# A new written-out instruction order and new PSUM banks for a fused conformer block

## The chip, the cores and the metric

The kernel runs on one core of a Trainium2 chip. The metric is device time in microseconds (us) of one launch; lower is better. A profile of one execution stands beside the times. Engines: TensorE (PE, with its weight loads PEld), VectorE (DVE), ScalarE (ACT), GpSimd (POOL), and SyncE (SP), which only issues transfers.

## The reference

One conformer block on x of shape (2, 4000, 144) in bf16, with 4 heads of 36 and a depthwise convolution over 5 steps:

```python
x = x + 0.5 * (silu(layernorm(x) @ w_ff1a) @ w_ff1b)          # 144 -> 576 -> 144
q, k, v = split_heads(layernorm(x) @ w_qkv)
p = softmax(q @ k.T * 36 ** -0.5)                             # 4000 x 4000 for each batch and head
x = x + merge_heads(p @ v) @ w_o
a, b = split(layernorm(x) @ w_pw1)
c = depthwise_conv(a * sigmoid(b), dw)                        # 5 taps along time
x = x + silu(c) @ w_pw2
x = x + 0.5 * (silu(layernorm(x) @ w_ff2a) @ w_ff2b)
return layernorm(x)
```

## The kernel before, in words

**Tiling.** The 8,000 tokens are cut into 16 chunks of 500 (eight to a batch), a chunk into 4 blocks of 125 tokens. A chunk's queries meet the keys of its batch in tiles of 64 keys. One score tile holds 64 keys of four heads by 500 queries, as four 64x64 matmuls side by side in the array (PS<-QT,KT), which fill two PSUM banks. Its exponent is taken in one of two ways: on ScalarE, one ACTIVATE Exp of 128x1000 (PT<-PS); or on VectorE, by arithmetic on the bits in five instructions (two PT<-PS 128x500 to int16, two PT<-PT 128x1000 on uint16, one PT<-PT product). The matmuls with V (PS<-PT,VA, 64x37) add into two PSUM banks of their own (6 and 7); one column of ones gives the softmax sum. A "q" matmul in the program is one of these 64-row quads, "f" is one with the full array.

**Around the attention.** Before a chunk can be attended, its first feed-forward (PS<-XT,WA; tanh on ScalarE, TH<-PS; product on VectorE, HT<-TH,PS; PS<-WB,HT; residual on VectorE, X<-PS,X), a layer norm and the projections to Q, K and V (PS<-XTQ,WQ and so on, copies QT, KT, VA) must be done. After a chunk's attention come the epilogue (QT<-PS, transposes with IDF, AN<-PS,RD), the output projection, a layer norm, the gated product (U), the convolution (PS<-U,DG, then SW), a projection, the second feed-forward and the last layer norm, whose XN is stored (out_dram<-XN).

**A layer norm** is bn_stats on VectorE (ST<-X), then seven instructions on GpSimd in the middle of the run: a TENSOR_SCALAR RS<-ST, a power RS<-RS,NHALF, a TENSOR_SCALAR RS<-ST, and four XN<-X,RS. At the start and the end of the run VectorE or ScalarE makes XN. A 32x32 transpose on VectorE (XN<-XN) and two sets of transfers through DRAM (rows<-XN, four transfers; XT<-rows or XTQ<-rows, two) turn it to columns. GpSimd also copies the edges of U between chunks (U<-U).

**Order.** A planner in the program (`Sched`, `pick` and the loop at the end) walks through all this work and records every instruction with its dependences; each step of the planner makes a block of instructions on one engine. `Rec.op` keeps, for each instruction, what it reads and writes. Then `Rec.reorder(ORDER)` puts the blocks of each engine into another order: `ORDER` has one string for each engine, and the i-th character is how many places the i-th recorded block goes forward or back (P is 0, Q is +1, O is -1; `~` begins a longer form). `PLACES` has one digit for each PSUM tile, the bank of six (0 to 5) in which it lies, or the first of a pair. `Rec.place` reads it. Waits are put in afterwards, by `reorder` and `finish`, from the dependences that the order leaves open, a tile's bank being free when the tile before it in that bank has been read. Each engine and SP then run their own list strictly in order: an instruction that waits holds all behind it on its engine.

```python
            for i, blk in enumerate(blocks):
                assert at[i + shift[i]] is None
                at[i + shift[i]] = blk
            lines[e] = [o for blk in at for o in blk]
```

All instructions are issued from one line of the program (L419 in the profile), so groups are told apart by their tiles.

Of the kernel before, what the change touches and what calls it, by code (L numbers as in the profile page):

```python
# [44 lines left out]
        "LMNLPRPKWOYFMNOVNOHXXMKOLNNNN[[_MMMTLLTKKKLJOOPRP`MO_OMNOMPQLLMRMMMPPPQOSYP[MOOISOLNPPIPSPTOLRNNWPNO"
        "QQMMPUQRN[QQQRJFPPPPJQQSPPKQQNPPPPVPPQOPVXOOPNDNPRROSVSYNFWMPYUPNDPJFPNPTOPYOLOPNQ[NLNRPMRLNNOPhUNZM"
        "MMNLNNPMMWYLPNZKNLMF[LPPSLVINLNOMWQNYPYPLQHKOSNORPGPPPS[OOLOOPPYLNNNVOMNOM^QMNTOO_KMMNOMPPLPNQOYL]RY"
        "LMKLMMPLY]KLNNQXMRXSLI[MDObNOENPMMNSNNQMMWNNNOSVNiKZNNQOTFNNOMXXUMMMM?TLLIYMQXXLLMMQZMJJ`ORLMUMKQYNL"
        "INPMMUVNLNOMYPMOORNNRUNKPNO_ROQLSSKMQMKPROLPSOORNOSOOOTVNNNNSNTMTMNNOVXNOMORLSNVXIMSYLMKLN^XYNLMNHMM"
        "WLLMXMNYMOLNNXMNXMMVMM[SLJLLZN^OLNNJUbLLLQNLPRGNNOOOPNRNOPPPeOOOOPSOOORROf`OPNO^@QDLJLMOLTKLTMTRKGMQ"  # L50
        "QNUOPNROYYPZOHNbILLLLbTLLSLLLLPLM_M[MMMMMcMMMMNLMOdZMNNNNIMMMMXMNNVOMKMMZNOUaMMMQMM]^HOMKNNNJZMKM[LM"
        "QgLLLMWMMMMU]LLLV^MQJMWTMHBHMZSKL[PLLZTMK_bMMIGbMPLPQMSVCKRKSMBINPPSPVOLOOOOZQNNS[MMMMNSMOMNO]aNNcMM"
        "MMMMMMNLNNNZWNZMZPNKPMYBENOPJYNNPMPQOLQNPPRRO[YQJNOPQOPXFPHPNOOOPWOOOOOOXPMTQOLOK^OXNNOMPPPLPPHQQNgR"
        "cOLQOMPNOOOOdRM@LdOJOIPIOOOJOOOOJOOPNUPNOOQQYLQ]NLZ[LLLdWKIKLLLWULE]LLLLLOMWRcKLLLNZM[PMMRILNKZJ`[JK"
        "MOLLUbKeJLLYKOUKMMMMMY=KMNNZNL^NLNNNNNN_NNNOQQNPTHNN_NLOOO^QMNPKO^QQM_JFPLOPJMNPPLPhMPROOPQOWOWNNNNU"
        "U?NO[HMTOOOCNOOOQO[OQOUOOOPHVORPYMGNPPMOVNN[QOVKPNZPGLOY]OPLOPPPBHOOORPRROR`OPWQNZCLNNPQZKMQETOJOMNU"
        "OOOOOPPPP[OOPNQNQRLMVZLOTNKPLLOOPPVPNOVOMRMOSLOOPPPPPZOWOMNNN]NLMPRTLNZUNLQMNYWNRAOPTOSHRNDQOPTOOPNP"
        "UOUQ_LROQQIQFNOYPNUKQNKTNKOQRSTNQNRXFQOQVQULMVEMPPP[PPPQODZcMPMMQINPKMPNOOOPRMNPPPQOZOOOOOQOMOOPXOOZ"
        "NNNNNN`NPWMXNNOPNKOCNOXPNOQOMZQMUOKXMZP[^XIMMOOKPABPJOPPPXOOQOPPPRIOPSOVSMOTKQUKLPNQNPXQOMROMPMQWQMU"
# [10 lines left out]
    "act": (  # L70
        "PPPPPPPPPPPPPRTNNOOPPQOPPPPPPXPNOSNNNNPPPPQOPPSPNOQZQORKRSLLOQQJPPPPQQNQOPPPPPPPPPQQQMPPQOPPPPPPPPRO"
        "OPQOPQQNPPPPPPPPPPPPPPPPPPPPPPPPPPPPPPPPPPPPPPPPPPPPPPPPPPPPPPPPPPPPPQOPPPROSNOOPPPPPPPPPQOPPPPPPPPP"
        "QOPPPPPPPPPPPQOPPPPPPPPPPPPQOPPPPPPPPPPPRPNPQOPPPPPRPNPPPPPPPPPPPPPPPPPPPPPPPPPPPPPPPPPPPPPPPPPPQOQQ"
        "NPPPPPPPPPPPPPPPPPPPPPPPPPPPPPPPPPPPPPPPPPPPPPPPPPPPPPPPPPPPPPPPPPPPPQOPPPPPPPPPPPPPPQOPPQOPPPPPPPPP"
        "PQOPPPPPPPPPPPPPPPPPPPPPPPPPPPROOPQOPPPPPPPPPPPPPPPPPPPQOPPPPQOPPPPPPPPPPPPPPPPPROOQQQMPPPPPPPPPPPPP"
        "PPPPPQOPPQOPPPPPPPQOPPPPPPPPPPQOPPQOPPPPQQQQQKQQNPPPPPPQOPPPPPPPPPPPPPPPQOPPPQOPPPPPPPPPPPPPPPPPPPPQ"
        "OPPPPPPPTOOOOROOPPPPPPPPPPPPPPPQOPQOPPPPPPPPPPQOPPQOPPPPPPPQOPPPPPPPPPPQOPPPPQOQOPPPPPPPPQOPPPPPPPPP"
        "QOPRPNQOPPPPPPPQOPPPPPPPPPPPPPPPPPPPPPQRNOPPPQOPPPPPPPQQNPPPPPPPPQOPPPPPPPQOQOPPQOPPPPPPPPPPQOPPPPPP"
        "PPPQOQOPPPPPPPPPPPPPPPPPPPPPPPPPQOPQQNPPPPPPPPPPPPPPPPPPPPROOPPPPPPPPPPPQQNPPPPPPPPQOPPPPPPPPPPPPPPP"
        "PPPPPQOPPPPPPPRPNQOPPPPPPPQOPPPPPPPPPPPPQOPPPPPPPPPPPPPPPPPPPPPPPPPPPPPPQOPPPPPPPPPPPPPPQOPPPPPPPPPP"  # L80
        "PPPPPPPPPPPPPPPPPPPPPPPPPPPPPPPPPQOSPNRNOQOUQNPMOPPPRORNQNPPPPPPQOROQQMPPPPPPQOPPPWORNNNOO"
    ),
# [2064 lines left out]
```

## Time and profile before

| what | value |
|---|---|
| runs | 875.77, 875.0, 875.19 us; median 875.19 |
| span of the profiled execution, first to last instruction | 873.9 us |
| its own time beside the span | not listed; the median of the runs is 1.3 us above the span |
| TensorE clock granted | 0.998 of full speed |
| instructions | PE 11,419, DVE 1,821, ACT 1,098, POOL 573 |
| DMA | 28.82 MB, mean 33 GB/s |

A group of the profile is read as: operation, tile written <- tiles read, shape, count, then busy time and mean ns of one, then the idle time just before and what ended it. Records of ScalarE and VectorE overlap a little where one follows another at once. A row of a timeline is start, duration (of a merged run of like instructions), engine, operation. Rows of a stage table give the stretch, its length, then busy us and count for PE, PEld, DVE, ACT and POOL, then granted clock, DMA share and GB/s.

### The profile page before, as it was taken

What the parts mean: (1) busy time and instruction counts of PE and PEld (TensorE: products, weight loads), DVE (VectorE), ACT (ScalarE), POOL (GpSimd) and SP (SyncE); (2) the same over time, 40 slices, a digit from 0 to 9 for tenths busy, and PEclk for the clock granted to TensorE, in tenths of its full rate; (3) what the DMA queues carried; (4) which work ended last, traced back from release to release, by engine and by line L of the source; (5) the groups of instructions that cost most, each with busy time, mean ns of one, the idle gap of its engine ahead of it and who ended that gap; (6) DMA issues with size and microseconds to landing.
All of it is one profiled execution on the core that took longest, in us unless ns stands there. A gap on an engine that the chain in (4) does not pass through costs nothing.

```text
span 873.9 us, 27051 instructions
## 1 busy us (share of the span) xinstructions
PE 844.3 (97%) x11419; PEld 385.8 (44%) x11419; DVE 824.8 (94%) x1821; ACT 845.4 (97%) x1098; POOL 292.8 (34%) x573
## 2 busy tenths in 40 slices
PE   8999999999999999999999999999999999999996
PEld 6543444334444434443444444445444433444465
DVE  7988999999999999999989999899999999999987
ACT  6799999999999999999999999999999999999985
POOL 6750350341325141152211552621314413022434
PEclk9999999999999999999999999999999999999999
DMA  4230101121121020212001120110111011001111
GB/s 100 49 62 29 23 17 44 33 67 30 29 52 39 17 50 11 45 22 47 23 4 29 24 56 17 30 30 16 37 31 24 21 31 21 19 15 38 28 26 35
DMA packets 114353, 28.82 MB, mean 33 GB/s; under 512 B 101090, under 2 KB 114230, under 8 KB 114230
## 3 DMA queue, kind: packets, MB, share of 16 engines
q1 hardware_dynamic: 112646, 26.39, 13.8%
q8 instruction: 90, 1.47, 0.7%
q10 hardware_dynamic: 1584, 0.69, 0.3%
q14 instruction: 33, 0.27, 0.1%
HBM read 13.44 MB, written 13.61 MB: 31 GB/s over the span
## 4 chain that ended last, share of the span: by engine, by line
ACT 59%; PE 25%; DVE 11%; POOL 4%; issue 1%; POOLq 0%; DVEq 0%
ACT PT L419 54%; PE PS L419 25%; ACT TH L419 5%; DVE PT L419 4%; POOL XN L419 2%; POOL RS L419 2%; DVE ST L419 2%; DVE X L419 1%; DVE XN L419 1%; DVE HT L419 1%; DVE U L419 0%; DVE KT L419 0%; DVE RS L419 0%; DVE AN L419 0%; DVE XT L419 0%
## 5 line engine op out<-in xcount | busy, mean ns | idle before, releaser
L419 ACT ACTIVATE PT<-PS 128x1000 bf16<-128x1000 f32 (+1 forms) x818 | 752.0, 1051 | 3.7 <-PE PS L419 2.8
L419 PE MATMUL PS<-QT,KT 64*64 64x500 bf16 x3968 | 419.9, 384 | 12.4 <-ACT PT L419 7.4
L419 PE MATMUL PS<-PT,VA 64*37 64x500 bf16 x4728 | 406.4, 372 | 1.6 <-DVE QT L419 1.0
L419 DVE TENSOR_SCALAR PT<-PS 128x500 int16<-128x500 f32 x380 | 250.2, 668 | 6.9 <-PE PS L419 5.1
L419 PEld LDWEIGHTS PS<-QT,KT 64*64 64x64 bf16 x3968 | 124.8, 104 | 232.0 <-ACT PT L419 132.2
L419 POOL TENSOR_SCALAR RS<-ST 125x4 f32<-125x4 f32 x130 | 37.8, 291 | 475.6 <-DVE ST L419 469.0
L419 PEld LDWEIGHTS PS<-PT,VA 64*37 64x37 bf16 x4728 | 142.7, 96 | 93.4 <-issue 13.6
L419 DVE TENSOR_SCALAR PT<-PT 128x1000 uint16<-128x1000 uint16 x380 | 154.2, 419 | 2.3 <-PE PS L419 1.0
L419 POOL TENSOR_SCALAR XN<-X,RS 125x144 bf16<-125x144 bf16 x260 | 144.7, 586 | 9.7 <-DMA out_dram<-XN 1.5
L419 DVE TENSOR_TENSOR PT<-PT 128x1000 bf16<-128x1000 bf16 x190 | 127.5, 674 | 0.9
L419 ACT ACTIVATE TH<-PS 128x500 bf16<-128x500 f32 (+3 forms) x194 | 102.8, 551 | 4.7 <-PE PS L419 4.5
L419 POOL TENSOR_TENSOR RS<-RS,NHALF 125x4 f32<-125x4 f32 (+1 forms) x93 | 92.8, 1002 | 33.5 <-DVE RS L419 27.9
L419 DVE SCALAR_TENSOR_TENSOR HT<-TH,PS 128x500 bf16<-128x500 bf16 (+1 forms) x135 | 81.0, 613 | 10.1 <-ACT TH L419 9.7
L419 PE MATMUL PS<-XT,WA 80*128 80x500 bf16 (+5 forms) x288 | 74.5, 364 | 4.2 <-DVE XT L419 1.0
L419 DVE BATCH_NORM_STATS2 ST<-X 125x6 f32<-125x288 bf16 x160 | 65.5, 446 | 1.6 <-DMA X<-in_x_dram 1.4
L419 DVE SCALAR_TENSOR_TENSOR X<-PS,X 125x288 bf16<-125x288 f32 (+1 forms) x128 | 56.6, 449 | 5.6 <-PE PS L419 4.3
L419 PE MATMUL PS<-WB,HT 128*125 128x144 bf16 (+1 forms) x640 | 52.6, 230 | 0.8 <-ACT HT L419 0.5
L419 PEld LDWEIGHTS PS<-WB,HT 128*125 128x125 bf16 (+1 forms) x640 | 44.3, 136 | 14.2 <-issue 4.3
L419 PEld LDWEIGHTS PS<-XT,WA 128*128 128x128 bf16 (+1 forms) x288 | 21.1, 97 | 37.7 <-issue 10.1
L419 POOL COPY U<-U 128x2 bf16<-128x2 bf16 (+1 forms) x54 | 12.0, 263 | 56.2 <-DVE U L419 56.2
L419 DVE STREAM_TRANSPOSE XN<-XN 128x320 f32<-128x320 f32 x54 | 27.0, 500 | 2.8 <-POOL XN L419 2.6
L419 PE MATMUL PS<-U,DG 128*128 128x250 bf16 (+6 forms) x204 | 28.8, 263 | 0.1
(95 smaller groups left out, 519.9 us busy)
## 6 DMA issues: line engine op xcount, KB each, us to landing
rows<-XN SPq DMA_DIRECT2D x216, 40.0 KB, 2.0
XT<-rows SPq DMA_DIRECT2D x56, 128.0 KB, 2.0
rows<-AN SPq DMA_DIRECT2D x60, 40.0 KB, 2.0
X<-in_x_dram SPq DMA_DIRECT2D x15, 140.6 KB
XTQ<-rows SPq DMA_DIRECT2D x26, 70.3 KB
out_dram<-XN SPq DMA_DIRECT2D x13, 140.6 KB
XT<-rows SPq DMA_DIRECT2D x56, 16.0 KB, 1.9
out_dram<-XN SPq DMA_DIRECT2D x3, 70.3 KB
```

The costliest lines, as they stand in the source:

```text
L419: ins = getattr(eng, o.name)(*o.a, **o.k)
```

## The change

The two tables get new contents: all five strings of `ORDER` and the digits of `PLACES`. The recorded instructions, their number, their operands except for the PSUM bank, and every other line of the program stay. The new order comes from a re-timing of the recorded program with mean intervals, in which an instruction of GpSimd has a price that depends on what VectorE runs beside it. Each string begins as before. Cut to the beginnings:

```diff
 ORDER = {
     "pe": (
-        "PPPPPPPPQOPPPPROQNPPRQPQLPPRPTPUPNIZOVOKVVL~OOKOK~OUHINSNLMMMOPNOJSOOL[I[KMYMKOGRNJHFKOOOE^NNN_dMKLM"
+        'PPPPPPPPQOPPPPROQNPPQQQRLRPQLSOSQNLYWXMQOXJ~O^JtG~O[IILRKKLLLNOQRRRTMTWCZCQMPAGGc>HKKLMOMG]MMM_gLJKKWbKH?KILDHjafGeGEIoKHNIIaOJJJJKVJKKK_ZJS'
 ...
     "act": (
-        "PPPPPPPPPPPPPRTNNOOPPQOPPPPPPXPNOSNNNNPPPPQOPPSPNOQZQORKRSLLOQQJPPPPQQNQOPPPPPPPPPQQQMPPQOPPPPPPPPRO"
+        'PPPPPPPPPPPPPPRSNNOPPQRNQNPPQOWORNTNLNPPPQRSTTUWIJVRUHLMGNPPQQQMPPPPQQNPPPQOPQQQQQQQQHPPPPPPPPPPPQOQQQMPPPPPPPPPPPPPPPPPPPPPPPPPPPPPPPPPPPPPP'
 ...
     "dve": (
-        "PUO[VM~P6~P6~P)~P6ILIKKLDKMJQRJJJKIKQKKLJKMKOLJWOILJHLJNQNPHFGNNNJMMMMBMWOIKIMINLMNOODNDPSPLORCFVSWC"
+        'PUO[VM~P2~P<~P6~P6ILIKKLDKMJQRJJJKIKQKKLJKMKOLJMMIMKMMJSOKNHIIKLLLLLLLLLWKOKTHYHLMPPPCRCQTPSSS=>SJV>MALRLZB:THHKKLEKKLLEMMJLNKKLOPLMPSOOQDPP'
 ...
     "pool": (
-        "PPPPPPPROOPPPSOPNPQQQQQQJPPPPPP_PPPPPJOOPQ[NKTMMOMNOSNUMNSNRNTKVNVMPLMPMROQTMOOTVMNNNOQTMOOQWMOOOSNN"
+        'PPPPPPPROOPPPROQNPPPPPPQORPQQQQJPPPPPQOPPVQNR[NKMOOOSNUMMPLTNPPQLQORSNRMRMSUMOPSOJOPPPQOPPPPROOPRRNRPLQOQOPPQOPPROQN'
 ...
     "sp": (
-        "PPQOPPPPQOPPPPPPPPPPPPPPWPWMNNNOPLPPPPPPQOPPPPPQRNOPPPPPQOPPQOPPPPPPPPPPPPPPPPPPPPPPPTOPNYNOWNNNNNNN"
+        'PPPPPPPPQOPPPPPPPPPPPQQNRPRMOPPPPPPSOOOPPQOPPPPPROOPPPPPQOPPSOOQNPPPPPROOPPPPPQOROOPPTOPNZNOUNNNNNNOTOTNNNOQOPPUOOOPNPPPPZOOOOOOOPNOPPPPPPPU'
 ...
 PLACES = (
-    "3054320451505435202310543130213550204405323242301405230054110122532155431241204124012410314032034023"
+    '30543204515054352123103401355024221105304541034523052303450014223451310452412041240124103140030241334102432040234013402430043213430243040224'
 ...
```

More of the change, by code (lines that the diff above doesn't have):

```diff
@@ L45 @@
[L45 to L59, printed above, removed]
@@ new lines @@
+        '5KMKCTZUIJ]JHIQ[SMKUGL^KLLMNPQMNOTPQUWJOINNSOPLQSPUOQQIQRUQQQLFQQQMPZPPPLPNOOOOhZORPUMIJMORYKIMNPM_NNRMNGPNQQNLPNUXNSNLNLOQSVOXX^OZ_MNGBGWKI'
+        'LLVPJQIKRNdNSVNLPMfN^MVNNNJMMM?VNNNa^YLDKKLWLZKKO]VJXFJbSLXYJGLQNHWNKWT5KNdXJNaQMULLN@KNTKMMYNLJOVPNOYJOLPYOaRJNPPIaSYOMDOOKOEQNJQRNRPJPPWPZ'
+        'MNNNOMTNNOM]OOOPNRPWX[^MHMOJENJSMNL[TOK_MNUYJMKb_LIMHLLTQMIMKOZKMPMSPNLNOQO]OOOOOQOMQQUMRPYHRPRVOSJE^MKOPNOPPM[^MMMWL[_KKKKKLJQ]aUKKVFKKKLUS'
+        'LJKUMPJPNPRO^TMYPMMJQMMMNNQOTO^OMPQLXPQKPTJOJLQQNXOOOOOZNNNOTNNPMXLOORNNNOVOOQNNU^MNNOTLNNNUUWNLMNZPNUjOMTNL=NRSQNGUOOOOOSDOQNSQIXLOOOOOOOZO'
@@ new lines @@
+        'OOOOUNPMMVYLPNRXJLVOJLW[LLOQJMMPNPRMY[RPKQKKOQNPRPGPPPQUQOLPQQQWJOOOOOZNPNOQNPMOO^bNNNOMO_LPNPJJL]MSLPKKQ`PMWGNLNNOWLX^OLI[NINIMNSMNLMYTNNOM'
+        'N[NNNORVN`OLNNQOUDNNOMZSLMMNSOZNKTLNOUcMNNOTFNNNWMWNLMOMXJXOJNOMNRaNKOPNOPNOOQRMQUMJPNOWQOPXKWQLQLJOQZJOQNNOUOMNNOVTNNNNQMUPWMNNP_LNQ]NQNPMQ'
+        'FZOW^ILHNNOXXGJMZWKK[JJKXLLSKL[LLWKOWLMXLLXYKILM]PT[JHMIQ^[JKUJLWPHLLNGMaPRMWMMNZMMMMMUMMMURMa[OLOPSC`KLMRJLUMJMNTPTLJMQQMYOPNQN]OPUMI`PLMPN'
+        'IWPLOLNNNN_WNNNQMMYLMeMMMMVLMMfMMMMOMSNNNNQSNOEVMNOMTMNW`MPNSNNNGWPNLNOMNSOSNTMNWcMMNNWMMMNSULLLT]M]QMUINCMNNOVIN[TMMTXNJ_`OLTESKLMRLNTV?KXM'
@@ new lines @@
+        'ROSPPEQU[]NDMMOLT^MKNUKINNUZMKMMM`bMMcLLLMMMMMNLNPKUXOSNGZLGQNLSZOVLMIOO[NJSO^KPMPNQNGPUZPNJOQQUGOKPMPPPPfOOOOOQRNLNORVTLaNJ[PLGPNGOZPKLNOPe'
+        'QOSPPJlYNNOMVRL9KcOIPHHRNOMZOOQSNLHMA]NOOOYR`Lb_KKX[JEJd`IEJHLHYTKEPDKKKY]LTZPGLIKL^LWWLLOHLM]aK^JLLcQMJJ`NWHRGMJFUHLLMXXLTIMMMUMKQRMZLOOOOO'
+        'OOOQ`MOQYMMNgNLPPKPQIPSGOZPQO`OGOGLQ^KKPQaPgIPHOPGROWN]NNNNTC>NN[INTOOOGNOOOQOPPPVOOOORNNPRPRMQNPPPS[OO_PPQHNPTYTMOIVQM@WNOPDbNNNQOQQNQ_NOFP'
+        'M^NKOPPQIVMPPGOSPIOaOOOOOOZOO_NOMPPLTPJPA[WOJOZPILNPNP^OFPMOOQTNOKNNPPPPPZOdPMOOKYOLNPJMWOYUQLTMKEWNQBNOPNSSOMNQOPTOOOOPPRZO^^NNNN]MWPCeJN]M'
@@ new lines @@
+        'EPH^C_NIKURLQNKXFGPBXPNYN]GNNKO^WNLQOLS_NOHOOWPR;QQ]KQJ[EXOfNKOHNOZHQGSMPJQKKPLOQQQSQSNPGWRTOPLTNTWQMMPTOVNOYTOWLOVPNWN]U^DNNNQHQ(LMYOOPRUOM'
+        'PNDQOROOPPPUSNORLRUSJOLRMSQRLMSPNQNXOPNRPQTKKPQVQRWOPQFSSO]LQORTOMOOXSNXOPQWRZLQaLOPASOO(KOOOZNNNNTNNUULLVKMXLNOMbN_MMMUQLLLLNX^NIMMOPTMSOCL'
+        'MQOPQOPXRNOMOQRNTPUROMSODOQOPQORUXNLOMNSOMN[PNWNOMRMMMMUVNYMSLLLMXSMMMNQTMTLOM]TOL[XNKSPIYNISQGUSEO_STJUMRPUJK>OMSUOKP[OKQSMRXKLOKNOVRNLQOLX'
+        '[NOMNOVLNLNNTMTVMMMTUSMMIRLQWPLQNNWOMVWNO`[ITIJMTMMNOMDPNQOUOOU_MV`LJMVQIMOIXNU`ENNUNTDGMMMPPSLPTLP_MNPNOSPMYNKYRXN[JRILEKRKQNLQOR_OQLQORKOP'
@@ new lines @@
+        'UPPSLNFXPNVNO]OSJMJPMSNPT`PWJX[_cJCLJKN^KDGLJ]LLNNN[SLFSK^KKLTMNOb^XNKNLMNOM@MNOTPNROHPRVQSPKTRPLGWPN]WNNUNLHMQWXKQ_LMENZKOPQ`NHNSSZWNSIGN@O'
+        'SVJXNUNOMOR`ZLO;cOMKWMYRMKILLPUOL@UMMPNOYaNNNOXTMJ[RKILMHOMX`WLLLMZLLLLNNNSOMUQQXRa]P[TN@EMKOOPNAPGPRXNNVNN^MMMMWQMNLNNNNUUNNPNYTJNSMNL[_QMQ'
+        'INOVPMGQKLMROVROLNO^PMO`NNRNOKOKXTM^JM^VLHMPRLNDXNS`N[DMNNOPNOPNAPQLSO^OSSOOLHQOMQOQRPJQRPMSQRRTTTOHRRTRPRSQRTRCSVP9QJNQRPQKPQSPPQRUOTGUN]PL'
+        'QHPRKvMMNRSLRMJMRNOMOPPQQNSSNRMRLCNPNPNOOOOUPNOOOPPPQOPQO'
@@ L69 @@
+        ''
     ),
     "act": (
-        "PPPPPPPPPPPPPRTNNOOPPQOPPPPPPXPNOSNNNNPPPPQOPPSPNOQZQORKRSLLOQQJPPPPQQNQOPPPPPPPPPQQQMPPQOPPPPPPPPRO"
[L72 to L75, printed above, removed]
@@ new lines @@
+        'PQOPPPQOPPQOPPQOPPPPPPPPPPPPPPPPPPPPPPPPPQOPPPPPPPPPPPPPPPPPTOPPQQKQQQMPPPPPPPPPPPPPPQOPQQNPPPPPQOPPPPPPPPPPPPQOPQQNPROQQQQQQIQQNPPPPPPPPPPP'
+        'PPPPPPPPPPPPQOPPPSORNNPPPPPPPPPPPPPPPPQQNPPPPPPPTOPNOROOPPPPPPPPPPPPPPPPPPPPPPPPPPPPPPQOPPQOPPPPPPPQOPPQQNPPPPPQOPPPPRORNOPPPPPPPPPPPPPQOROQ'
+        'NPPSQNNPPPQQQQQQJQOPQQNQQQMPPPPPPPPPPPQOSOOQQQLPPPPPPPPQOPPPPPPPPPROOPPPPPQOPQOPPPPPPPPPPPPPPPQOPPPPPPPPPPPPPPPPPPPPPPPPPPPPPPPPPPQQQMPQQNPP'
+        'PPPPPPPPPPPPPPPPPPPPPQOPPPPPPPPPQQNPPPPPPPPQOPPPPPPPPPPPPPQQNPPQQQMPPPPQQNRPNQOPQOPPPPQOPPPPPPPPPPPQRNQQQLPPQOPPPQQQQLPPPPPPPPPPPPPQRPQLPPPP'
@@ new lines @@
+        'OREQNQQNQSQOSQOQVVWOPNKN@OPQOPQOROORRNNQOPQOSSPNQTPPPRSQUMQQRR>QQQQQQEPPWOOOPNOOVPNOPNVNOOOOOQOPUOOVNNNORNSMPNQOPPSPSMPMPPPPPPRPNPPPPVOQUMVO'
+        'PLPPRPEPQO[OTOMOMNQOUOKTOQ[MJOOOOOOOPTUOKVPQKPJQNQRRORPRRSURLNRRNQQQQQQQQQQQSQRTQZPQTQGPRPWJP#PPRVQWQQNWHPNBOOOQOPSOOOROOXOiNOROMNRHNPRLNNPN'
+        'SNNNNSNNNPWOOOOOPQQQQQQHP`SNNNNOOPNOOTOMO[RKNNOOOTNPTRVOVHHOMNTNOOOQOPPPPPPPQSNPNPWROMTMOMNPQOPSOOOQOQOPPQSQOLQOPROQQMPPPPQQNPPSSNNRMQNPPRPQ'
+        'QLPRRRN]PJOPNOOOOOOOQOQOPQOPPPPPPQOSOPNPPPQOPPTRWMMQLWOLRMVMUVKLNLMOdSPPLLOOWNNOMOMNNOPQMPPTPNPNPPQRPMPRSOMQNQQNRPNRORNOPPPPPPPPPUOPNROMRfNP'
@@ new lines @@
+        'MSOSNKMUMO]OMNORNFMMTOURKLPLQOPRTNSMRMMPPPPPROQNSPNOPPPPPPQOQOTOSTMNLOPSOOOPROOQOSOOOQOPPgPNOPNRSNTKNSJMULTLMMNLPROOROVNOOOPQMPPPPPPUQNPMOXP'
+        'PMOOOUOMPNTNOOOPQOYOOOTOMNNNPPQQQSPRJQRPKPPUPNPPMQQNTOPRTNQOSVROUDKNNOPPQOPPPPPPPQQNPRORNOQOPQOPPQRNRNRRMTQTRJUKROJVPSPTOQTTPHTRPLTRS<MMTOPP'
+        'MQOQOSORRRLZQOPQRNOPROSVR>NLPQMPQORPNPPPPPPQOQOVOOPNPNPPRPQQRPRTWPSSPSWSQRRSVRYQ?7O?QQNQQJPPPPPPPQOPQOPROhQOPROOQGNPNOOOOPPPRPJMOPPPRPNROOPP'
+        'QOUQNQOLPQOPPQOPQQRMOSPUQRZSIPTHOIQMQSKTNPMOPPPVOPXOOOQOHRNNQRTOLPNRYQVQOQQUSFSEIMRRRMQLWSNNQMSQURIKTOLOSNPNQOQOROOPROQNPQSPMRPMTQSZM[PRKUMV'
@@ L105 @@
+        ''
     ),
     "sp": (
-        "PPQOPPPPQOPPPPPPPPPPPPPPWPWMNNNOPLPPPPPPQOPPPPPQRNOPPPPPQOPPQOPPPPPPPPPPPPPPPPPPPPPPPTOPNYNOWNNNNNNN"
-        "VOWNNNNPMOPVOZNOMNNOOSNNNPPZOPNOOOOOOOPQSNOOPPQQN"
+        'PPPPPPPPQOPPPPPPPPPPPQQNRPRMOPPPPPPSOOOPPQOPPPPPROOPPPPPQOPPSOOQNPPPPPROOPPPPPQOROOPPTOPNZNOUNNNNNNOTOTNNNOQOPPUOOOPNPPPPZOOOOOOOPNOPPPPPPPU'
+        'VNNNNNOPPPPPPPROO'
+        ''
     ),
@@ new lines @@
+    '52305240425042105245024504250425042504250424052404250425023504250324302350243034203530143025243054204403250424052505320524054205320524502405'
+    '24052404250424052505250424052405240253003414314002254411240124210412041204131043103420532033051035103515301035130402430243024301430143034210'
+    '43013402430342034201340315401320341204021402140214021402143104140134021402140214021401340214012042104310431043104212403154301140124240204214'
+    '12041204021402104213412041204120412024230034243024310430243024502352130340214021411341040043214021402140214021401340214020412041104331340214'
@@ new lines @@
+    '12041214013401340214020412140204102402141200421025052504205240441330052502401214023401340101305224120402140204120412041204124124120041134021'
+    '43425301503510351341043141204203532034013401340214012043025301530153015301530130104502431004321403153013010032143024301404302430243020425431'
+    '04002431340234023410241334013410431330105301530153015031003513513234011340104331043141042041104310430143013531043310431041204313401340120412'
+    '04120412041204013402140214024024303420243024302430342034203402340234024030232430523055310430234032404204350425024025054204203450320525042044'
@@ L130 @@
+    '24052505240520305312030542045204250524052504240420524052504240504225043251403034202403430242104303402235042034203430235024203430242034034203'
+    '24023520350235103104253413401350235024302430204313401042341204120402014021420402140240124121412040214102402140423040323413561445520322602013'
+    '24143254105304421103341250153354054253016503'
 )
```

65 lines of the change are left out of this document (11 added, 54 removed).

## The prediction

> **What bounds the kernel now.** I read the profile page first, then the busy time by stage, the waits of each engine, and the timeline where an engine falls short. The page:
>
> ```profile
> span 873.9 us, 27051 instructions
> PE 844.3 (97%) x11419; PEld 385.8 (44%) x11419; DVE 824.8 (94%) x1821; ACT 845.4 (97%) x1098; POOL 292.8 (34%) x573
> ACT 59%; PE 25%; DVE 11%; POOL 4%; issue 1%; POOLq 0%; DVEq 0%
> ```
>
> Three engines are nearly full, and the chain that ended last runs 59% through ScalarE (ACT), 25% through TensorE (PE), 11% through VectorE (DVE) and 4% through GpSimd (POOL). The same instructions run after the change, so a gain can only come out of idle time, stretched instructions or TensorE's changes of array shape. By stage (time, PE, weight loads, DVE, ACT, POOL busy):
>
> ```profile
> 17.00:50.00 33.00, 30.49 (x320) 16.45 (x317) 31.15 (x81) 27.81 (x50) 23.65 (x49) 1.00 0.23 48
> ...
> 75.00:540.00 465.00, 457.16 (x6306) 196.80 (x6308) 447.66 (x949) 462.20 (x571) 145.08 (x277) 1.00 0.15 32
> 540.00:565.00 25.00, 23.47 (x300) 10.37 (x292) 21.61 (x46) 24.43 (x33) 17.36 (x28) 1.00 0.09 18
> 565.00:825.00 260.00, 252.39 (x3499) 109.75 (x3495) 252.85 (x529) 259.93 (x321) 72.20 (x143) 1.00 0.12 26
> ...
> 840.00:874.00 34.00, 26.82 (x318) 23.03 (x315) 28.02 (x102) 22.14 (x58) 11.84 (x16) 0.95 0.13 33
> ```
>
> From 75 to 825 us ScalarE shows 2.80 + 0.57 + 0.07 = 3.4 us without work. The room lies at the ends: 5.2 us in 17 to 50, and 11.9 us after 840.
>
> ```profile
> PE PS L419 <- ACT PT L419: 8.3, 30, 0.5
> PE PS L419 <- DVE PT L419: 2.1, 7, 0.8
> ```
>
> These are TensorE's waits between 50 and 840 us (total, times, longest). They are waits for a PSUM bank that the exponent on ScalarE, or VectorE's exponent, has not yet read. So in the middle TensorE and ScalarE hold each other, and speeding up one alone is only partly paid.
>
> **The change, part by part.** I read the shift tables against the blocks of the kernel before. At another place stand 2,307 of 2,855 blocks on TensorE (median two places), 270 of 1,093 on ScalarE, 1,250 of 1,689 on VectorE, 72 of 125 on GpSimd and 76 of 157 on SP; 409 of 1,724 PSUM tiles get another bank. Matched with the instructions of the trace, the first 16.9 us stay as they are.
>
> *Changes of array shape on TensorE.* Counting neighbours in the two orders, matmuls of another kind (64-row quads beside full-array ones, or the small V forms) follow each other 768 times before and 746 times after, 22 fewer. The price:
>
> ```profile
> 406.49 0.38 PE L419 MATMUL PS<-QT,KT 64*64 64x500 bf16 x4
> 406.70 0.38 PE L419 MATMUL PS<-PT,VA 64*37 64x500 bf16 x4
> ...
> 410.00 0.41 PE L419 MATMUL PS<-QT,KT 64*64 64x500 bf16 x4
> 410.34 0.59 PE L419 MATMUL PS<-XTQ,WK 72*128 72x500 bf16 x2
> 410.90 0.41 PE L419 MATMUL PS<-QT,KT 64*64 64x500 bf16 x4
> ```
> ```profile
> L419 PE MATMUL PS<-XTQ,WK 72*128 72x500 bf16 (+1 forms) x68 | 19.2, 366 | 0.0
> ```
>
> Four quads take 0.21 us when quads follow (406.49 to 406.70) and 0.34 when a full matmul follows: 0.13 for the change. Back, two full matmuls step by 0.59 - 0.37 = 0.22 each, 0.44 in all, and the quads come after 0.56: 0.12, which may hold a wait. So 22 x 0.125 = 2.75 us less on TensorE. What covers it: ScalarE, wherever the chain does not run through TensorE. I take the chain's 25%, -0.7 us; ends -2.75 and 0. The Trainium skill, TensorEngine Tiling (Array Packing), section Key Properties, says that changing the tiling mode drains the engine. The skill's TensorE: Matmul & The Clock Gate, section Step-by-step, counts 128 cycles for a drain, which at 2.4 GHz gives an estimate of 0.053 us and 1.2 us for the 22, against 2.75 by the rows; the measured rows decide here.
>
> *The stretch from 17 to 50 us.* ScalarE's waits there, and the chain:
>
> ```profile
> ACT TH L419 <- PE PS L419: 2.8, 5, 1.4
> ACT PT L419 <- PE PS L419: 1.0, 2, 0.8
> ACT XTQ L419 <- PE PS L419: 0.6, 2, 0.3
> ACT VA L419 <- PE PS L419: 0.6, 1, 0.6
> ```
> ```profile
> 17.29 1.01 POOL RS L419
> ...
> 29.67 0.50 POOL XN L419
> 30.21 0.51 DVE XN L419
> ...
> 38.58 8.00 PE PS L419 x90
> ```
>
> GpSimd carries the chain from 17 to 30 us and its order is unchanged up to 35 us, so those 13 us stay. Behind them the new order brings the copies of XTQ, K and Q on ScalarE forward by 5 to 11 places and puts tanh blocks back by 1 to 7; on TensorE the long run of 92 full-array matmuls is broken up, with quads in between; the exponent that waited 0.8 us changes places with the next. Of the 5.0 us waited I take that 0.8 and a little more, -1.0. Ends: -5.0 (all of it) and +1.4, once more the longest wait seen there, since the tanh blocks put back feed VectorE. The large memset of U2 moves five places back on GpSimd; the work it then stands behind is not on the chain after 38.6 us, so it costs nothing, and its own reader comes later than 50 us.
>
> *The GpSimd pile-up at 543 us.* Four layer norms stand there in a row, with VectorE beside the first:
>
> ```profile
> 544.56 1.57 POOL L419 TENSOR_SCALAR RS<-ST 125x4 f32<-125x4 f32 x1
> 546.23 2.79 POOL L419 TENSOR_SCALAR XN<-X,RS 125x144 bf16<-125x144 bf16 x4
> ...
> 559.50 0.23 POOL L419 TENSOR_SCALAR RS<-ST 125x4 f32<-125x4 f32 x1
> 559.84 1.87 POOL L419 TENSOR_SCALAR XN<-X,RS 125x144 bf16<-125x144 bf16 x4
> ```
> ```profile
> 544.71 0.74 DVE L419 TENSOR_SCALAR PT<-PT 128x1000 uint16<-128x1000 uint16 x2
> ...
> 545.37 0.67 DVE L419 TENSOR_TENSOR PT<-PT 128x1000 bf16<-128x1000 bf16 x1
> ```
>
> The same 125x4 operation takes 1.57 us beside VectorE's PT passes and 0.23 without; four XN take 2.79 against 1.87. The change swaps the third and the fourth layer norm, so the fourth, on the chain, ends some 4.3 us sooner, and the third, which feeds a store, later. SP gets that store into the gap in which it waits for rows to land:
>
> ```profile
> 562.28 2.55 SPq L419 DMA_DIRECT2D rows<-XN  x4
> 566.23 0.82 SPq L419 DMA_DIRECT2D XT<-rows  x2
> ```
>
> Behind it on SP stand the XT loads; the store's input would end by about 562, before the load could go at 566, so it holds nothing up. At stake is ScalarE's 0.57 us of this stage; I take -0.4; ends -0.57 and +0.5 should the store's layer norm come later than that.
>
> *The rest of the middle.* Nothing but a shuffle by a place or two; each of the queues, SP's 76 moved blocks of two or four DMAs included, has the order of its inputs nearly as before. At stake are 2.87 us of ScalarE's idle time; I take -0.5; the loss end is the first rival below.
>
> *The tail.* On VectorE the four XN of one store move eleven places back, behind the last residuals, and three residuals of other chunks 15 to 48 places back:
>
> ```profile
> 864.57 1.00 DVE L419 TENSOR_SCALAR XN<-X,ST,RS 125x144 bf16<-125x144 bf16 x4 [0.22 <-POOL RS L419]
> 867.40 0.45 DVE L419 SCALAR_TENSOR_TENSOR X<-PS,X 125x288 bf16<-125x288 f32 x1
> 869.36 0.55 DVE L419 TENSOR_SCALAR XN<-X,ST,RS 125x144 bf16<-125x144 bf16 x2 [0.75 <-POOL RS L419]
> ```
> ```profile
> 866.35 0.84 PE L419 MATMUL PS<-WB,HT 128*125 128x144 bf16 x10 [0.34 <-ACT HT L419]
> ```
>
> The last residual could start at 867.19 instead of 867.40: -0.2. The moved 1.0 us then fills the 0.75 us that VectorE waits before its last XN, so its excess, +0.25, lands on the end, and its store leaves with the last ones. Taken as 0; ends -1.5 and +1.5 (the 1.0 us and half a microsecond of store, or the same won by the deferred residuals).
>
> **Sum.** -0.7 - 1.0 - 0.4 - 0.5 + 0 = -2.6 us on a span of 873.9. The median of the runs, 875.19, lies 1.3 above the span for what stands around it; I carry that over: 872.6 us, 0.3% faster.
>
> **Rivals.**
> *Score tiles behind VectorE (slower).* Of 818 score tiles, 167 were written into a bank that a VectorE instruction had last read; with the new banks 181 are, 14 more. Such a wait costs 2.1/7 = 0.3 us in the row above. If each of the 14 waits, and every wait reaches ScalarE, that is +4.2 us; with half of the gains still there, 875.2 + 4.2 - 1.3 = 878.1. For it speaks that VectorE is 94% busy and seldom early; against it that only seven such waits showed for 167 tiles. It decides from about 15 waits on, where it eats the 2.6 us and 0.2% more.
> *ScalarE covers everything (no change).* The 2.75 us won on TensorE turn into waiting for ScalarE, the order of the ends is worth nothing: 875. For it speaks the 99.9% of ScalarE in 565 to 825 us; against it the 25% of the chain on TensorE.
> *The stretched GpSimd work shrinks (much faster).*
>
> ```profile
> L419 POOL TENSOR_SCALAR XN<-X,RS x260: 454/503/1447, 18.7 to 837.2; 125x144 bf16<-125x144 bf16 x130
> L419 DVE TENSOR_SCALAR PT<-PT x380: 353/411/667, 74.1 to 834.9; 128x1000 uint16<-128x1000 uint16 x190
> ```
>
> Least, median and longest differ threefold on GpSimd and twofold on VectorE. If the new order sets the two apart so that VectorE's passes lose half of 411 - 353, that is 380 x 0.029 = 11 us of VectorE; by its 11% of the chain 1.2, and with the pile-up's 3 x 0.9 us of XN gone as well, 872.6 - 1.2 - 2.7 = 868.7. Against it: the number of operations of both is the same, and they must overlap somewhere. The Trainium skill, SBUF — State Buffer, section "SBUF: two separate sides", says that GpSimd and VectorE's two-port operations share one port pair, locked for a whole instruction while the loser blocks; by that rule the stretch is waiting, and an order can remove it or add to it. The row at 544.56, held until VectorE's pass of 545.37 is over, agrees.
>
> **How the numbers follow.** Forecast (870.7 to 873.4) 0.37; much faster 0.13; no change 0.21; slower 0.29. Two measurements of this kernel that differ by less than 0.2% (1.75 us) can't be told apart, so faster holds 0.37 + 0.13 = 0.50, the same 0.21, slower 0.29. The range reaches from a little below the much faster case to a little above the slower one, 867 to 879.5; the forecast alone would span 869.5 to 874.
>
> **What would show it.** Right: ScalarE's waits of 17 to 50 us below 4.5 us; changes of shape won show as less TensorE busy time (841 to 843 us); the third of the four layer norms near 543 us ends and SP's loads behind it go some 4 us sooner. Wrong: TensorE's waits for VectorE's PT above 4 us in all, new ScalarE idle time between 75 and 825 us, or a last store that ends the program later than 4.5 us after its issue.

## The result and the profile after

The new kernel takes 870.13 us (median of 5 runs, 870.06 to 870.58), the one before 875.27 us beside it (5 runs, 875.0 to 875.82): ratio 0.9943, 95% interval 0.9931 to 0.9955. That is 5.1 us faster, inside the range, and twice the 2.6 us that the prediction summed up. (In two of the experiments below single executions took 1,921 and 2,642 us; the ratios leave them out.) The profiled execution took 870.43 us with a span of 868.6. Its page, the lines that answer to those of before:

```profile
span 868.6 us, 27054 instructions
PE 839.5 (97%) x11419; PEld 383.2 (44%) x11419; DVE 825.2 (95%) x1821; ACT 843.3 (97%) x1098; POOL 288.7 (33%) x573
ACT 61%; PE 30%; DVE 7%; POOL 1%; issue 1%; DVEq 0%; POOLq 0%
```

The shares of VectorE and GpSimd in the chain fell (11 to 7% and 4 to 1%); ScalarE and TensorE now carry 91% of it. TensorE is 4.8 us less busy for the same matmuls. By stage (time, PE, weight loads, DVE, ACT, POOL busy):

```profile
17.00:50.00 33.00, 31.23 (x355) 17.27 (x354) 31.77 (x82) 29.06 (x52) 24.28 (x50) 1.00 0.24 49
...
75.00:540.00 465.00, 457.46 (x6354) 199.04 (x6342) 450.52 (x956) 464.12 (x575) 142.53 (x282) 1.00 0.15 32
540.00:565.00 25.00, 24.03 (x305) 9.66 (x305) 22.68 (x46) 25.00 (x34) 14.57 (x27) 1.00 0.23 51
565.00:825.00 260.00, 252.31 (x3519) 107.84 (x3512) 253.08 (x530) 259.91 (x320) 73.75 (x143) 1.00 0.11 23
...
840.00:874.00 34.00, 20.54 (x249) 17.90 (x247) 22.73 (x87) 16.89 (x43) 11.20 (x15) 0.89 0.08 23
```

ScalarE's time without work from 75 to 825 us fell from 3.4 to 1.0 us. Where the 5 us come from is read better from the start of the n-th of ScalarE's 818 exponents in the two traces (times as in the timelines):

| exponent | before, us | after, us | lead, us |
|---|---|---|---|
| 1st | 19.4 | 19.4 | 0.0 |
| 9th | 47.1 | 45.2 | 1.9 |
| 76th | 112.3 | 110.3 | 2.0 |
| 161st | 198.9 | 194.6 | 4.3 |
| 201st | 235.7 | 231.6 | 4.1 |
| 501st | 531.9 | 526.4 | 5.4 |
| 551st | 582.3 | 576.8 | 5.5 |
| 818th, the last | 837.0 | 830.8 | 6.1 |
| end of the span | 873.9 | 868.6 | 5.3 |

So three places gain: 1.9 us in the opening, some 2 us between the 76th and the 201st exponent (the 161st stands at a peak: the 160th leads by 2.6 us, the 172nd by 3.7), some 2 us over all the rest of the attention. The stage of the pile-up (501st to 551st exponent) gains 0.05 us. After the last exponent 0.8 us are given back.

**The opening.** One row of VectorE's timeline and three of GpSimd's, of before and then of the new kernel (start, duration, operation; in brackets the idle time ahead of it and who ended it):

```profile
33.64 0.16 DVE L419 TENSOR_SCALAR RS<-ST 125x2 f32<-125x2 f32 x1
```
```profile
27.85 2.32 POOL L419 TENSOR_SCALAR XN<-X,RS 125x144 bf16<-125x144 bf16 x4
...
33.89 2.06 POOL L419 TENSOR_TENSOR RS<-RS,NHALF 125x2 f32<-125x2 f32 x3 [3.69 <-DVE RS L419]
...
36.30 1.01 POOL L419 TENSOR_TENSOR RS<-RS,NHALF 125x4 f32<-125x4 f32 x1
```
```profile
30.31 0.16 DVE L403 TENSOR_SCALAR RS<-ST 125x2 f32<-125x2 f32 x1
```
```profile
27.63 2.33 POOL L403 TENSOR_SCALAR XN<-X,RS 125x144 bf16<-125x144 bf16 x4
...
30.56 1.64 POOL L403 TENSOR_TENSOR RS<-RS,NHALF 125x2 f32<-125x2 f32 x2 [0.57 <-DVE RS L403]
...
32.56 1.01 POOL L403 TENSOR_TENSOR RS<-RS,NHALF 125x4 f32<-125x4 f32 x1
```

Up to 30 us GpSimd runs as before. Then it waited 3.69 us for a variance step of VectorE (RS<-ST), and now 0.57, because VectorE's new order has that step at 30.31 and not at 33.64 us; the next layer norm's power starts 3.7 us sooner (36.30 to 32.56). But the chain of before does not run through this wait. Two of its rows, then rows of the new chain:

```profile
38.17 0.37 DVE X L419
...
46.60 0.58 ACT XTQ L419
```
```profile
31.43 0.76 POOL RS L403
...
36.34 0.51 DVE XN L403
...
37.61 7.57 PE PS L403 x90
...
45.20 5.49 ACT PT L403 x6
```

Before, the chain from 30.21 us to the row at 38.17 runs through VectorE alone; in the new kernel GpSimd carries it from 31.43 to 36.3 us, with the norm that comes sooner. VectorE then releases TensorE's long run 1.0 us sooner (38.58 before), the run is 0.4 us shorter (8.00 before), and the copy XTQ on ScalarE no longer stands between that run and the ninth exponent, another 0.5 us. These three make the 1.9 us; which of the moved blocks earns the first of them is not shown.

**The middle.** ScalarE's and TensorE's waits, in the new kernel (17 to 50 us for ScalarE, 50 to 840 for TensorE: total, times, longest):

```profile
ACT PT L403 <- PE PS L403: 1.9, 2, 1.8
ACT KT L403 <- PE PS L403: 1.1, 2, 0.7
ACT TH L403 <- PE PS L403: 0.8, 2, 0.5
```
```profile
PE PS L403 <- ACT PT L403: 7.4, 25, 0.6
PE PS L403 <- DVE PT L403: 1.3, 6, 0.3
```

TensorE's two rows fell by 1.7 us together, less than the middle gained. What changed more: between 50 and 836 us I took, for each ScalarE instruction, the time from the start of the one before it, less the lowest tenth of that time for the same form. In the trace of before 56 instructions are over 0.1 us late by this measure, 11.2 us in all; in the new one 34, with 6.3 us. All of them waited for TensorE; 44 of the 56 and 28 of the 34 are exponents, whose score tile came late, most of the others tanh. That difference, 4.9 us, covers the middle's 4.3 us (9th to 818th exponent).

### The profile page after: what moved, and what is told of

It reads as the page before. It is cut to its first block, busy times and chain, and to the rows that moved or that the text cites. A ratio compares the mean times of both kernels' runs of the same rounds, so it can differ in the third digit from the quotient of the medians.

```text
span 868.6 us, 27054 instructions
## 1 busy us (share of the span) xinstructions
PE 839.5 (97%) x11419; PEld 383.2 (44%) x11419; DVE 825.2 (95%) x1821; ACT 843.3 (97%) x1098; POOL 288.7 (33%) x573
## 4 chain that ended last, share of the span: by engine, by line
ACT 61%; PE 30%; DVE 7%; POOL 1%; issue 1%; DVEq 0%; POOLq 0%
ACT PT L403 56%; PE PS L403 30%; ACT TH L403 5%; DVE PT L403 3%; DVE ST L403 1%; DVE X L403 1%; DVE XN L403 1%; DVE HT L403 1%; DVE QT L403 1%; POOL RS L403 0%; POOL XN L403 0%; DVE DG L403 0%; DVE SW L403 0%; ACT XT L403 0%; ACT L403 0%
## 5 line engine op out<-in xcount | busy, mean ns | idle before, releaser
L403 POOL TENSOR_SCALAR RS<-ST 125x4 f32<-125x4 f32 x130 | 36.8, 283 | 502.9 <-DVE ST L403 496.4
L403 PEld LDWEIGHTS PS<-PT,VA 64*37 64x37 bf16 x4728 | 139.8, 96 | 96.0 <-issue 15.2
L403 PE MATMUL PS<-XT,WA 128*128 128x500 bf16 (+5 forms) x288 | 74.4, 364 | 1.8 <-ACT PT L403 0.8
L403 PE MATMUL PS<-IDF,QT 128*125 128x128 f32 x128 | 23.0, 302 | 0.8 <-ACT PT L403 0.4
```

The costliest lines, as they stand in the source:

```text
L403: ins = getattr(eng, o.name)(*o.a, **o.k)
```

## Experiments

Lines of the two tables say nothing to a reader, so the edits below name blocks. Times are medians; each run has its own runs of the kernel before beside it.

**The opening alone, seam at 48 us.**

```diff
-ORDER, PLACES: before
+ORDER, PLACES: new for blocks that start before 48 us in the new kernel, before for the rest
```

> The new order and banks for all blocks that start before 48 us, the old ones behind them; the last stores are those of before. The theory that the gain is made place by place (1.9 us in the opening, by when the 51st exponent starts, 4.2 us between there and the last exponent, 1.0 us given back by the last stores) expects 875.2 - 1.9 = 873.3 us. The rival, that what the opening gains is taken back by the first stretch in which the old order waits for something that does not come sooner (the loads, GpSimd's masks and norms), expects 874.8 us or more.

878.48 us, ratio 1.004 (1.0028 to 1.0052): slower than before, which neither theory meant (the rival's "874.8 us or more" takes it in by its wording alone). The lead of 1.9 us is there up to the 13th exponent and turns into 3.1 us of delay by the 21st; from there to the last exponent the delay stays between 3.09 and 3.15 us. So the place of the loss is the seam, where TensorE waited twice. Its rows, then the stages (the column behind the counts is the granted clock):

```profile
49.78 0.32 PE L398 MATMUL PS<-WQKV,XTQ 72*64 72x72 bf16 x8 [1.24 <-ACT PT L398]
...
51.82 1.06 PE L398 MATMUL PS<-WQKV,XTQ 72*64 72x72 bf16 x28 [1.18 <-DVE VA L398]
```
```profile
50.00:52.00 2.00, 0.82 (x21) 0.32 (x16) 1.92 (x6) 1.00 (x1) 1.04 (x3) 0.74 0.14 23
52.00:54.00 2.00, 2.00 (x34) 1.04 (x35) 0.86 (x2) 0.14 (x1) 1.69 (x4) 0.50 0.12 21
54.00:56.00 2.00, 2.00 (x18) 1.25 (x10) 1.00 (x2) 2.00 (x3) 1.02 (x3) 0.50 0.36 62
56.00:58.00 2.00, 2.00 (x19) 0.60 (x18) 1.19 (x3) 0.72 (x2) 0.42 (x2) 0.56 0.25 72
58.00:60.00 2.00, 2.00 (x24) 0.66 (x22) 0.85 (x2) 1.85 (x4) 1.82 (x4) 1.00 0.25 72
```

2.4 us of waiting were followed by some 7 us at half clock (1 us of the first stage, four in full, nearly 2 of the fourth); together they are enough for the 5 us of loss. This run says nothing of the opening's worth; it was repeated with a seam at which both orders had issued the same blocks.

**The opening alone, seam at 94 us.**

```diff
-ORDER, PLACES: before
+ORDER, PLACES: new for blocks that start before 94 us in the new kernel, before for the rest
```

> As the run with the new opening alone, but with the seam at 94 us, where the blocks issued so far are the same ones in both orders on every engine (at 48 us the two differed by three blocks, and that run lost 5.1 us at its seam between 50 and 60 us and then ran the old order at the old pace, 3.1 us late to within 0.1 us for 780 us). If the opening's gain is its own, and only the seam cost it, the lead at the 76th exponent (2.0 us) lasts to the end: 874.9 - 2.1 = 872.8 us. If the old order takes the gain back: 874.5 us or more.

873.39 beside 875.31 us, ratio 0.9979 (0.9968 to 0.9989): -1.9 us. In its trace the lead is 2.55 us at the 76th exponent and 2.56 at the 451st (0.5 of it was there at the first exponent, which starts at 18.7 to 19.4 us from one execution to another). To 0.2 us, a lead made in the opening is neither lost nor enlarged by the old order behind it.

**All but the opening.**

```diff
-ORDER, PLACES: before
+ORDER, PLACES: before for blocks that start before 50 us, new for the rest
```

> The old order and banks for all blocks that start before 50 us, the new ones behind them, the last stores too. Place by place: 875.2 - 4.2 + 1.0 = 872.0 us. The rival, that the middle only gains because the opening left the engines in another state to each other, expects 874 us or more. The two halves together, this one and the opening alone, should add up to the whole 5.1 us by the first theory.

872.2 beside 874.88 us, ratio 0.9974 (0.9965 to 0.9982): -2.7 us, near the 872.0 of the first theory. With the opening's 1.9 that makes 4.6 of the 5.1 us.

**One stretch with more changes of array shape.**

```diff
-ORDER, PLACES: before
+ORDER, PLACES: new for the blocks between 94 and 198 us of the new kernel only
```

> The kernel before with the new order and banks only for the blocks issued between 94 and 198 us of the new kernel; at both ends the blocks issued so far are the same ones (but for one of GpSimd and one of SyncE at 198 us). This stretch makes 9 changes of array shape more than before (777 in all for 768), and in the profile of the new kernel ScalarE gains 2.0 us in it, as exponents that come late to their scores fall from 15 with 3.6 us to 7 with 1.6 us. The theory that the gain is in where the steps lie, not in the number of changes, expects 875.3 - 2.0 = 873.3 us. By the number of changes at the 0.063 us that the dummies measured: +0.6, 875.9 us. If a seam costs it: 874.5 us or more.

874.11 beside 875.2 us, ratio 0.9987 (0.9978 to 0.9996): -1.1 us, between the two expectations for the place-by-place theory and a seam. The lead grows from 0.6 us at the 51st exponent to 2.5 at the 161st, near the 2.0 expected, and falls to 1.5 by the 201st. Of this 1.0 us, 0.3 goes at the 162nd, as in the new kernel itself; 0.7 goes at the 166th, where the new kernel loses 0.1: that is the seam of 198 us. So the stretch is faster with 9 changes more than before; by their number it should have been slower.

**The longest stretch.**

```diff
-ORDER, PLACES: before
+ORDER, PLACES: new for the blocks between 198 and 829 us of the new kernel only
```

> The kernel before with the new order and banks only for the blocks between 198 and 829 us of the new kernel; the opening, the first 198 us and the last stores are those of before. 23 changes of array shape fewer (745 for 768). From the profiles ScalarE gains 2.1 us in this stretch: 873.2 us. By the changes alone at 0.063 us each: -1.4, 873.9 us. If the stretch gains only what the earlier ones hand on: 875 us.

872.83 beside 875.2 us, ratio 0.9974 (0.9963 to 0.9984): -2.4 us, near the -2.1 of the place-by-place theory. The estimate by the 23 changes alone, -1.4, lies within the run's interval (-1.4 to -3.2), at its edge.

**What a change of shape costs.** Two kernels with 44 added matmuls each:

```diff
+    R.extra = lambda eng, bk: eng.matmul(PSV[:, bk, CH:512], lhsT=IDENT[:, :], rhs=IDENT[:, 0:12], start=True, stop=True,
+                                         skip_group_check=True)
...
                         eng.wait_ge(self.sems[lane], v)
+                    if e == "pe" and i in EXTRA:      # 44 places
+                        self.extra(eng, EXTRA[i])
                     ins = getattr(eng, o.name)(*o.a, **o.k)
```

> The new kernel with 44 small matmuls added between 70 and 815 us, full-array ones of 12 columns into the unused last columns of the bank that the next step writes; each stands between two quarter-array matmuls of the scores, so 88 changes of array shape are added. Their results are not used. If each change costs its 0.125 us on the path: 44 x (0.25 + 0.03) = +12 us, 882 us. If, as the prediction took it, a quarter of it lies on the path: +3 us, 873 us. If ScalarE covers it: 870.1 to 870.6 us.

> The same 44 small matmuls added to the new kernel, but each between two full-array matmuls, so no change of array shape is added. What this run is above 870.1 us is the price of the instructions alone, at most 44 x 0.03 to 0.06 = 1.3 to 2.6 us if TensorE's time lies on the path everywhere, and 0.3 to 0.7 us if a quarter of it does. The difference of the other run to this one is the price of the 88 changes.

875.67 us between quarter-array matmuls (ratio to the kernel before 1.0003, 0.9993 to 1.0012) and 870.14 between full-array ones (0.994, 0.9928 to 0.9953). The 88 changes cost 5.5 us, 0.063 each (0.047 to 0.079 by the two intervals). TensorE's rows around one of the dummies:

```profile
310.79 0.37 PE L406 MATMUL PS<-QT,KT 64*64 64x500 bf16 x2
311.10 0.18 PE L2103 MATMUL PS<-IDENT 128*128 128x12 bf16 x1
311.21 0.41 PE L406 MATMUL PS<-QT,KT 64*64 64x500 bf16 x4
```

Quad, dummy, quad step by 0.31 and 0.11 us, where quad to quad takes 0.21. Summed over the 44 places TensorE is 8.67 us longer, over the 44 full-array places 1.30: (8.67 - 1.30) / 88 = 0.084 us for a change on TensorE, of which three quarters reach the end. The 1.30 us among full-array matmuls do not. The Trainium skill, TensorEngine Tiling (Array Packing), Key Properties, names the drain; the 0.053 us estimated from the skill's 128 cycles is short of the 0.084 measured on TensorE, which decides.

**Late scores moved forward.**

```diff
 TensorE's order, at 14 places
-<block that is not needed yet>
 PS<-QT,KT   (a score its exponent waits for)
+<block that is not needed yet>
```

> The kernel before with 14 score blocks moved one block earlier on TensorE, nothing else: those whose exponent waited for them although their own inputs and their bank were free before the block ahead of them began (3.0 us of ScalarE's late starts in the trace of before). TensorE then has 772 changes of array shape in its place of 768. The theory that the middle's gain comes from scores issued sooner for ScalarE expects -1.5 to -3.0 us: 871.9 to 873.4 us. The theory that it comes from fewer changes of shape expects +0.1 to +0.5 us: 875.0 to 875.4 us.

875.56 beside 875.31 us, ratio 1.0001 (0.9992 to 1.001): nothing. ScalarE at one of the 14 places, before and then with the move:

```profile
197.74 0.86 ACT L419 ACTIVATE TH<-PS 128x500 bf16<-128x500 f32 x2
198.89 4.59 ACT L419 ACTIVATE PT<-PS 128x1000 bf16<-128x1000 f32 x5 [0.30 <-PE PS L419]
```
```profile
198.65 1.00 ACT L398 ACTIVATE PT<-PS 128x1000 bf16<-128x1000 f32 x1
199.96 3.69 ACT L398 ACTIVATE PT<-PS 128x1000 bf16<-128x1000 f32 x4 [0.30 <-PE PS L398]
```

The wait of 0.30 us is gone ahead of one exponent and stands, 0.30 us long, ahead of the next. Of the steps from one exponent's start to the next, 11 became over 0.1 us shorter, 2.0 us in all, and 10 longer, 2.2 us; the late starts sum to 11.2 us before and 11.3 with the moves. So the lateness was handed on; that it belongs to TensorE's whole run up to that point is a reading of this, not shown by itself.

**Five joins.** On the new kernel with the old tail (below), five single full-array blocks put next to another full-array block:

```diff
 TensorE's order, at 5 places
 <full-array block>
+<full-array block>
 PS<-QT,KT or PS<-PT,VA  (one or two blocks)
-<full-array block>
```

> The new kernel with the old tail, and five single full-array blocks of TensorE moved past one or two score blocks to stand next to another full-array block: 736 changes of array shape in place of 746. Chosen where the inputs were there and the consumer did not wait in the profile. At 0.063 us a change: 869.3 - 0.6 = 868.7 us. If, as with the 14 score blocks, what one exponent gains the next one loses: 869.1 to 869.5 us. If a moved score now comes late: above 869.5 us.

869.74 us, ratio 0.9937 (0.9924 to 0.9949), 0.45 us above the 869.29 it started from (beside its own runs of before 5.5 us faster, that one 5.6). Three of the joins (at 64, 405 and 552 us) cost 0.16 to 0.25 us each in the trace, two (at 634 and 799 us) nothing. A further 0.5 us at 227 us is a row load that came late:

```profile
PEld PS L398 <- DMA XTQ<-rows: 0.9, 1, 0.9
```

None of the joins is near there, so that half microsecond is not theirs. Ten changes fewer, and no gain.

**GpSimd's order alone.**

```diff
 ORDER["pool"]
-before
+new
```

> The kernel before with GpSimd's new order alone (the fourth layer norm's variances before the third's at 543 us among it); all other engines and the banks as before. The prediction's third step expects -0.4 us, 874.9 us; if GpSimd's order is what the change gains by, 873 us or less; if it is worth nothing by itself, 875.3 us; if GpSimd now comes late for an order that counted on the old one, 875.5 us or more.

876.31 beside 875.2 us, ratio 1.0017 (1.0008 to 1.0026): slower by 1.1 us. The ten runs fall into six of 875.8 to 876.4 us and four of 877.4 to 877.7; the trace is of one of the four. It shows a gain and a loss. Up to the 801st exponent it leads by 1.1 us, with 0.7 of that at the 533rd (563 us, the pile-up), of which 0.36 goes again at the 586th and 587th. At the 804th and 805th it loses 3.2 us:

```profile
POOL U L398 <- DVE U L398: 18.4, 1, 18.4
```
```profile
820.87 0.51 DVE L398 STREAM_TRANSPOSE XN<-XN 128x320 f32<-128x320 f32 x1 [1.77 <-POOL XN L398]
```

In the new order GpSimd copies an edge of U ahead of a layer norm. VectorE's old order makes that U late, at 816 us, so GpSimd stands 18.4 us, the norm starts late and VectorE's transpose waits for it. TensorE, which then waits for VectorE's exponent, stands 1.86 us, and about 3.4 us at half clock follow:

```profile
822.65 0.62 PE L398 MATMUL PS<-QT,KT 64*64 64x500 bf16 x2 [1.86 <-DVE PT L398]
```
```profile
822.00:824.00 2.00, 1.35 (x12) 0.35 (x12) 1.86 (x5) 0.13 (x1) 1.82 (x4) 0.63 0.25 43
824.00:826.00 2.00, 2.00 (x18) 1.03 (x18) 0.84 (x2) 1.49 (x2) 1.66 (x3) 0.51 0.26 47
```

So part of the 3.2 us is the clock's and not the order's own. Whether the six shorter runs were spared the half clock is not shown, as no trace of them was taken.

**The tail.** Two kernels: the new one with the old order behind 829 us, and the new one with one store's work moved:

```diff
 after 829 us, all engines
-ORDER, PLACES: new
+ORDER, PLACES: before
```
```diff
 VectorE, behind the statistics at 859.55 us
+XN<-X,ST,RS x4          (140 KB store)
 X<-PS,X ... RS<-ST,RS   (nine instructions)
-XN<-X,ST,RS x4
 SyncE
+out_dram<-XN 140.6 KB
 out_dram<-XN            (two smaller stores)
-out_dram<-XN 140.6 KB
```

> The new order and banks up to 829 us, the end of the attention, and the old order of what follows: the 140 KB store then leaves 3.8 us ahead of the end as before and not with the last ones. If the late 140 KB store costs what the traces show at the end (last issue to the program's end 1.1 us longer), 870.1 - 1.1 = 869.0 us. The rival, that the end is set by the computation and the old tail is the slower one in that, expects 870.1 us or more.

> The new kernel with one step moved: the four normalisations on VectorE that make the 140 KB store run four steps earlier (before the residual add at 859.7 us and not behind the last variance), and its store is issued ahead of the last two of SyncE. VectorE has no free time there, so what it does behind that place but ahead of the last four comes up to 0.9 us later, and then catches up. If the late store costs the 1.1 us: 869.0 to 869.6 us. If the computation sets the end: 870.1 to 870.9 us.

869.29 us (868.81 to 869.61; ratio 0.9935, 0.9923 to 0.9947) and 869.64 us (869.24 to 869.86; 0.994, 0.9927 to 0.9953). The intervals of the ratios overlap that of the new kernel, and beside their own runs of before (874.88 us) they gain 5.6 and 5.2 us against its 5.1, so times alone do not part them; the traces do. From the start of the last exponent to the end the new kernel takes 37.8 us, the one with the store moved 37.3, the one with the old tail 36.8 (the kernel before 36.9). End of the chain and span, the new kernel first, then with the one store moved:

```profile
862.19 1.14 DVE XN L403 x5
863.32 0.23 DVEq L2101
```
```profile
span 867.3 us, 27054 instructions
...
863.18 0.32 DVE XN L398
863.50 0.23 DVEq L2096
```

VectorE ends at 863.55 in the one and 863.73 in the other, later; yet the program ends 5.1 us after it in the one and 3.6 in the other. The transfers between 866 and 868 us say why (last column GB/s, share of the DMA engines beside it):

```profile
866.00:867.00 1.00, 0.00 (x0) 0.00 (x0) 0.00 (x0) 0.00 (x0) 0.00 (x0) 0.50 0.30 96
867.00:868.00 1.00, 0.00 (x0) 0.00 (x0) 0.00 (x0) 0.00 (x0) 0.00 (x0) 0.50 0.05 14
```
```profile
866.00:867.00 1.00, 0.00 (x0) 0.00 (x0) 0.00 (x0) 0.00 (x0) 0.00 (x0) 0.50 0.04 13
867.00:868.00 1.00, 0.00 (x0) 0.00 (x0) 0.00 (x0) 0.00 (x0) 0.00 (x0) 0.50 0.00 0
```

In the new kernel 110 KB still move in these two microseconds, when all engines have stopped, and 13 KB in the other: the stores are done a microsecond later. By the medians the one moved store is worth 0.5 us, the old tail 0.8. The version with the old tail has the lowest median of this study.

## Why the prediction was right, and where it was not

The sign held and the rivals stayed away; the size was half of what came. At 870.1 us the new kernel lies just below the 870.7 to 873.4 us of the forecast itself; the range of 867 to 879.5 us is so wide that lying in it says little of the mechanism. TensorE's busy time fell further than named, to 839.5 us (841 to 843). TensorE's waits for VectorE's exponent fell to 1.3 us in 6 times (2.1 in 7 before), so *score tiles behind VectorE* did not happen. *ScalarE covers everything* is refuted by the dummies: of the 8.67 us that they add to TensorE 5.5 reach the end. *The stretched GpSimd work shrinks* is not what happened: VectorE's PT<-PT average 417 ns (419 before), and GpSimd's XN are the same to the nanosecond:

```profile
L403 DVE TENSOR_SCALAR PT<-PT 128x1000 uint16<-128x1000 uint16 x380 | 153.1, 417 | 1.0
L403 POOL TENSOR_SCALAR XN<-X,RS 125x144 bf16<-125x144 bf16 x260 | 144.7, 586 | 8.3
```

| step | predicted, us | measured, us | from |
|---|---|---|---|
| stretch of 17 to 50 us | -1.0 | -1.9 | seam at 94 us |
| changes of shape, 22 fewer | -0.7 | up to -1.4 | dummies, 22 x 0.063; lies inside the other rows |
| GpSimd pile-up | -0.4 | 0 | 501st to 551st exponent |
| rest of the middle | -0.5 | -4.3 with the changes of shape | 9th to 818th exponent |
| tail | 0 | +0.8 | old tail |

*The opening* was mis-sized. The waits of ScalarE came out as named (3.8 us, below the 4.5), the 13 us under GpSimd did stay, and the copy XTQ brought forward paid 0.5 us. But the step took its size from ScalarE's one wait of 0.8 us and did not read the chain behind those 13 us, which VectorE alone carried for 8 us up to TensorE's run while GpSimd stood 3.69 us for it; that run starts 1.0 us sooner and is 0.4 us shorter. The whole was within the ends given.

*The changes of shape.* The price was too high by half (0.125 for 0.084 us on TensorE), the share that reaches the end too low (25% of the chain for 75%); the two errors partly cancelled. But the count is not the mechanism: the stretch from 94 to 198 us gains 1.1 us with 9 changes more, and ten changes fewer by five joins gained nothing, as three of the moves had a price of their own. Of the -22, -8 lie ahead of 94 us, +9 up to 198 and -23 behind.

*The rest of the middle* is the term that failed. It set the stake at ScalarE's 2.87 us of idle time and spoke of a mere shuffle. Idle time was the wrong measure: an exponent's record lasts some 1.0 us, but the next one starts 0.9 us after it (4.59 us for five in the row at 198.89), so 0.1 us of each late start hides under the record before. Counted by starts, 11.2 us stood at stake, and the new order won 4.9 of them. The 14 moved scores show that single late scores, moved by one block, do not win them; that the order as a whole does is argued from this, and which of the 2,300 moved blocks do it was not taken apart. Whether the order or the banks carry it stays open as well: no run has the new order with the old banks, the reverse, or the new order of a single engine other than GpSimd.

*The pile-up.* The step came as told: ScalarE's stage is full (25.00 of 25), and the XT loads behind the third norm start at 557.49 in place of 566.23 us, 8.7 sooner, of which 5.4 are the lead that the kernel had by then. GpSimd's order alone shows its worth, 0.7 us at that place and 0.3 left fifty microseconds later; in the new kernel nothing is left of it.

*The tail* had the mechanism and the sign of its excess right, and the size at zero. That its loss runs against the two larger gains brought the sum nearer to the forecast, which is luck. The sign set down for it came true: the last issues on ScalarE's queue start 5.3 us before the end (863.26 us), against 4.2 before (869.68).

The parts measured alone sum to -1.9 - 1.1 - 2.4 + 0.8 = -4.6 us; the missing 0.5 is less than the 0.7 us that the stretch ending at 198 us loses at its seam, and less than the interval of each part.
